# The first unit's softmax by tiles, and a new hand-written order for the opening of an attention and channel-mix kernel

## The chip, the cores and the metric

One core of a Trainium2 chip runs the whole kernel. The metric is the time of one execution in device microseconds, the median of three runs. The profile shows one execution of its own. Engines are named as in the profile: PE (matrix products), DVE (vector), ACT (activations), POOL (GpSimd), SP (the queue that issues the transfers).

## What is computed

Local attention over 4 batches of 768 tokens with 8 heads of 64, then a channel mix on the 512 features of each token:

```
for each chunk of 32 queries:
    k_full = concat(mem_k, k[chunk_start-16 : chunk_end+8])      # v_full the same
    a = softmax(q_chunk @ k_full.T / 8);  out = a @ v_full
x      = out as (batch, 768, 512);  x_prev = x shifted by one token
xk, xr = mu_k*x + (1-mu_k)*x_prev,  mu_r*x + (1-mu_r)*x_prev
k = relu(xk @ w_k);  v = (k*k) @ w_v;  r = sigmoid(xr @ w_r)
return r * v
```

w_k is 512 x 1024, w_v 1024 x 512, w_r 512 x 512; all are given as 64-bit floats.

## The kernel before

The tokens are worked in 12 units of 256, each of two tiles of 128. For a unit `u` the operations carry these names; the tile is `t` = 2u or 2u+1:

- `qk`, `vw`: loads of queries and keys, and of values, of a tile (672 and 512 KB).
- `s`: the scores of both tiles on PE, into one PSUM tile of two banks (line 430). `max`, `sub`, `exp`, `sum`, `norm`: the softmax on all 16 groups of 64 keys at once, each one instruction on 1024 elements per partition (lines 443 to 465; `sum` is a reduction, an addition and a reciprocal). `max` first writes a large negative number over the keys that don't exist at a batch's ends.
- `t`: transposes on PE; `bd.0`, `bd.1`: two copies that spread the transposed weights into a block-diagonal tile; `a`: the product with the values; `x`: the copy into the unit's token matrix `xT`.
- `mix`, `xh`, `xl`: the blend with the shifted tokens, and its split into a high part (fp32r) and a low part. For unit 0 the blend is a product on PE with diagonal matrices (`dg0`, `dg1`, eight ACT instructions each, line 346, from the identity `id` and `mu`). For later units `df` (line 593) takes the difference of a token and its predecessor and `mix` (line 603) does four multiply-adds on DVE for each of the two blends; the second blend is written over `df`.
- `h`, `g`, `v`: the products with w_k, w_r and w_v, each as three products of high and low parts (lines 654, 630). `sig` is the sigmoid of `g`; `relu`, `sq`, `kh`, `kl` the square of the rectified `h` and its split. From unit 3 on (`FAST`) the v product is done in seven parts (line 961) with sums of weights made on DVE.
- `w0` to `w9`: chunks of the weights of 1 MB: 0 and 1 are w_r, 2 to 5 w_k, 6 to 9 w_v. `load`; `mag` (ACT), `low` and `join` (DVE) make 32-bit floats of the 64-bit ones; `hi` and `lo` split them. In unit 0 `h0.n` needs chunk 2+n alone and `g0.n` chunk n alone, so that products start before all weights are there; `v0.n` needs chunk 6+n.

A planner orders everything. Its list `FIRST`, written out by hand, gives the opening operation by operation, each with its engine; each engine and the SP queue do theirs in that order. Behind the list a greedy planner with prices per operation and due times from PE's order goes on. PE's order from unit 1 on is fixed in `te_order`. Buffers are rings with few places: four of `big` (loads of `qk` and weights), six of `x4`, three of `vw`, one score tile `s`, two PSUM banks `tp`, four PSUM banks `m`. Where the planner foresees that PE idles early on, warm-up products on zeros are put in (line 1088).

PE's opening order before is `s0 s1 t0 t1 a0 a1`, `mix0.0 mix0.1 t2 t3 s2 a2 a3`, `h0.0` to `h0.3`, `t4 t5 s3 g0.0 g0.1 a4 a5 g1.0 g1.1`, then `h1` and `v0`.

Of the kernel before, what the change touches and what calls it, by code (L numbers as in the profile page):

```python
# [1139 lines left out]
```

## Time and profile before

| | us |
|---|---|
| runs | 399.12, 399.76, 399.77 (median 399.76) |
| the profiled execution | 398.94 |
| its span, first to last instruction | 397.2 |
| PE busy | 388.1 (98%) |
| DVE busy | 323.2 (81%) |
| ACT busy | 215.2 (54%) |
| POOL busy | 15.9 (4%) |

The span is what the trace covers; 1.74 us of the profiled execution lie around it. The granted clock of TensorE is 1.00 throughout. Busy shares are means over the whole span; the opening, which the change touches, is read from its own stretches.

### The profile page before, as it was taken

What the parts mean: (1) busy time and instruction counts of PE and PEld (TensorE: products, weight loads), DVE (VectorE), ACT (ScalarE), POOL (GpSimd) and SP (SyncE); (2) the same over time, 40 slices, a digit from 0 to 9 for tenths busy, and PEclk for the clock granted to TensorE, in tenths of its full rate; (3) what the DMA queues carried; (4) which work ended last, traced back from release to release, by engine and by line L of the source; (5) the groups of instructions that cost most, each with busy time, mean ns of one, the idle gap of its engine ahead of it and who ended that gap; (6) DMA issues with size and microseconds to landing.
All of it is one profiled execution on the core that took longest, in us unless ns stands there. A gap on an engine that the chain in (4) does not pass through costs nothing.

```text
span 397.2 us, 10852 instructions
## 1 busy us (share of the span) xinstructions
PE 388.1 (98%) x4803; PEld 357.6 (90%) x4803; DVE 323.2 (81%) x561; ACT 215.2 (54%) x340; POOL 15.9 (4%) x14
## 2 busy tenths in 40 slices
PE   7889999999999999999999999999999999999996
PEld 3579889888988989989989989989989999989995
DVE  1888989998789999789879879779779779478446
ACT  1867797714642864457457466357358364344440
POOL 2243020000010000000000000000000000000000
PEclk9999999999999999999999999999999999999999
DMA  8999894011063260142142142142130130100101
GB/s 304 412 352 355 268 362 133 8 69 39 2 229 110 102 246 3 55 151 98 55 138 110 54 174 73 54 148 99 55 109 2 53 108 2 53 2 2 54 0 53
DMA packets 13054, 46.63 MB, mean 117 GB/s; under 512 B 1488, under 2 KB 1872, under 8 KB 12496
## 3 DMA queue, kind: packets, MB, share of 16 engines
q1 hardware_dynamic: 13008, 45.95, 31.9%
q8 instruction: 37, 0.61, 0.6%
q14 instruction: 9, 0.07, 0.1%
HBM read 39.65 MB, written 6.29 MB: 116 GB/s over the span
## 4 chain that ended last, share of the span: by engine, by line
PE 93%; DVE 3%; ACT 2%; DMA 1%; issue 0%; SPq 0%; DVEq 0%
PE ph L654 33%; PE pr L630 17%; PE pv L630 8%; PE pa L961 6%; PE pb L961 6%; PE px L509 6%; PE pc L961 5%; PE s L430 4%; PE pd L961 3%; PE pt L492 3%; PE xf L562 2%; DMA qk<-in_qk_dram 1%; ACT k L346 1%; DVE sm_sb L443 1%; DVE e L447 1%; DVE o L985 0%
## 5 line engine op out<-in xcount | busy, mean ns | idle before, releaser
L654 PE MATMUL ph<-xh,wkh 128*128 128x256 f32 x384 | 106.2, 277 | 0.0
L654 PE MATMUL ph<-xl,wkh 128*128 128x256 f32 x384 | 106.0, 276 | 0.0
L654 PE MATMUL ph<-xh,wkl 128*128 128x256 f32 x384 | 106.0, 276 | 0.0
L654 PEld LDWEIGHTS ph<-xh,wkh 128*128 128x128 f32 x384 | 72.1, 188 | 0.2
L654 PEld LDWEIGHTS ph<-xl,wkh 128*128 128x128 f32 x384 | 72.1, 188 | 0.0
L654 PEld LDWEIGHTS ph<-xh,wkl 128*128 128x128 f32 x384 | 72.1, 188 | 0.0
L742 ACT ACTIVATE k<-ph 128x512 f32<-128x512 f32 x48 | 28.6, 598 | 71.9 <-PE ph L654 71.8
L917 DVE TENSOR_TENSOR khl<-k,khl 128x512 fp32r<-128x512 f32 x63 | 42.2, 687 | 25.4 <-ACT khl L316 24.4
L630 PE MATMUL pr<-wrh,xh 128*128 128x512 f32 x96 | 39.1, 408 | 0.0
L630 PE MATMUL pr<-wrl,xh 128*128 128x512 f32 x96 | 37.6, 392 | 0.0
L630 PE MATMUL pr<-wrh,xl 128*128 128x512 f32 (+1 forms) x108 | 37.6, 366 | 0.0
L316 ACT CAST khl<-k 128x512 fp32r<-128x512 f32 x43 | 26.4, 622 | 7.5 <-PE pb L961 2.5
L630 PE MATMUL pv<-wvh,khl 128*128 128x512 f32 (+1 forms) x97 | 30.3, 389 | 0.0
L749 ACT ACTIVATE k<-k 128x512 f32<-128x512 f32 x47 | 29.5, 632 | 1.3
L509 PEld LDWEIGHTS px<-aTz,vw 128*64 128x64 f32 x768 | 23.4, 138 | 3.4 <-issue 2.4
L509 PE MATMUL px<-aTz,vw 128*64 128x64 f32 x768 | 25.0, 223 | 1.1 <-DVE aTz L318 1.1
L318 DVE CAST khl<-k 128x512 fp32r<-128x512 f32 x32 | 13.1, 423 | 15.6 <-ACT k L749 15.2
L316 ACT COPY aTz<-pt 64x512 f32<-64x512 f32 x34 | 19.1, 580 | 12.0 <-PE pt L492 11.1
L701 ACT ACTIVATE sg<-pr 128x512 f32<-128x512 f32 x24 | 14.3, 599 | 19.4 <-PE pr L630 19.3
L961 PE MATMUL pc<-wtbig,khl 128*128 128x256 f32 x204 | 24.6, 276 | 0.0
L630 PEld LDWEIGHTS pr<-wrh,xl 128*128 128x128 f32 x108 | 20.3, 188 | 4.6
L961 PEld LDWEIGHTS pc<-wtbig,khl 128*128 128x128 f32 x204 | 23.8, 188 | 0.0
(110 smaller groups left out, 757.3 us busy)
## 6 DMA issues: line engine op xcount, KB each, us to landing
qk<-in_qk_dram SPq DMA_DIRECT2D x24, 672.0 KB, 6.1
vw<-in_vw_dram SPq DMA_DIRECT2D x24, 512.0 KB, 4.8
out_dram<-o SPq DMA_DIRECT2D x23, 256.0 KB, 2.1
raw<-in_w_k_dram SPq DMA_DIRECT2D x4, 1024.0 KB, 8.0
raw<-in_w_v_dram SPq DMA_DIRECT2D x4, 1024.0 KB, 6.6
raw<-in_w_r_dram SPq DMA_DIRECT2D x2, 1024.0 KB, 5.9
out_dram<-o SPq DMA_DIRECT2D x2, 128.0 KB, 1.7
id_sb<-in_ident_dram SPq DMA_DIRECT2D x1, 64.0 KB, 6.8
```

What stands on the lines that cost most here:

```text
L316: e.copy(dst, src)
L318: e.tensor_copy(dst, src)
L430: nc.tensor.matmul(s5[CHUNK * j : CHUNK * (j + 1), h, c, r, :], q4[z, r, j, :], k3[z, r, STEP * j : STEP * j + NK], start=True, stop=True,)
L492: nc.tensor.transpose(p[:, n * P : (n + 1) * P], e[:, n // 2, c, n % 2, :], id_sb)
L509: nc.tensor.matmul(p3[64 * h : 64 * h + 64, 2 * g : 2 * g + 2, CHUNK * j : CHUNK * j + CHUNK], v[:, g, h, j, :], a[:, h, g, j, :], start=True,
L630: nc.tensor.matmul(p[:, a : a + step], x, w[:, a : a + step], start=start, stop=stop and a + step == DM)
L654: nc.tensor.matmul(z, w, x[:, k], start=start, stop=stop)
L701: nc.scalar.activation(T["sg", u][:, c * DM : (c + 1) * DM], T["pr", u, c], AF.Sigmoid)
L742: e.activation(r, T["ph", u, f], AF.Relu)
L749: e.activation(q, q, AF.Square)
L917: e.tensor_sub(T["al", u, name], src, T["ah", u, name].bitcast(F32))
L961: nc.tensor.matmul(p, l[:, i], r[i], start=i + k == 0, stop=i == FT // 2 - 1 and k == 2)
```

## The change

Four things change. The softmax of unit 0 is done tile by tile: `s0`, `max0`, `sub0`, `exp0`, `sum0`, `norm0` work on the first tile's eight groups and a second set with the letter b on the other's; the second tile's scores go to the two `tp` banks, in two pieces. Unit 2 (`EACH`) has its exponential in 16 instructions on ACT, one for each group, that take the scaled maximum as bias (`neg2` on DVE makes it) and give the group's sum as well; the subtraction and the reduction are gone. From unit 3 on the blend is made without `df`: four ACT instructions `old` scale the preceding token by 1-mu, for each of the two blends, and four DVE instructions add mu times the token. And `FIRST` is another list: in it the loads of queries and values stand ahead of those of weights, `dg0` and `dg1` stand elsewhere, `norm1` and the low parts of three chunks are on DVE in place of POOL, `x1` is on ACT, and more such. PE's order changes in that `s0b` comes behind `s0`, and `s2` ahead of `t3`. Of the lists the first ten lines are shown.

```diff
+EACH = (2,)
...
 FIRST = """
-qk1@dma qk0@dma s0@pe max0@dve sub0@dve mu@dma w3.load@dma w3.low@dve w3.mag@act w3.join@dve exp0@act sum0@dve id@dma
-norm0@dve dg0@act dg1@act qk2@dma qk3@dma s1@pe t0@pe t1@pe bd0.0@act vw1@dma w3.hi@dve w3.lo@pool bd1.1@act vw0@dma
-bd0.1@dve bd1.0@act w2.load@dma a0@pe a1@pe x0@act max1@dve sub1@dve w2.mag@act x1@dve w2.low@dve w2.join@dve
-mix0.0@pe exp1@act w4.load@dma sum1@dve w4.mag@act xh0.0@act qk4@dma w4.low@dve mix0.1@pe norm1@pool t2@pe xl0.0@dve
-qk5@dma w4.join@dve bd2.1@dve w2.hi@act xh0.1@act vw2@dma bd2.0@act t3@pe bd3.0@act w4.hi@act w2.lo@pool w4.lo@pool
-bd3.1@dve vw3@dma xl0.1@dve w5.load@dma w5.mag@act w0.load@dma s2@pe max2@dve w1.load@dma qk7@dma sub2@dve w5.low@dve
-w5.join@dve w0.low@dve exp2@act sum2@dve vw4@dma a2@pe a3@pe x2@act x3@act w5.hi@act w5.lo@dve h0.0@pe h0.1@pe
-w1.low@dve w0.mag@act h0.2@pe h0.3@pe w1.mag@act qk6@dma w0.join@dve w0.hi@act relu0.0@act norm2@dve t4@pe bd4.0@act
-relu0.1@act sq0.1@act vw5@dma sq0.0@act kh0.0@act t5@pe w0.lo@dve s3@pe g0.0@pe relu0.3@act w1.join@dve w1.hi@dve
-relu0.2@act bd4.1@act bd5.1@act sq0.3@act w7.load@dma w7.mag@act bd5.0@act w1.lo@dve g0.1@pe sq0.2@act a4@pe x4@act
...
+qk0@dma mu@dma id@dma qk1@dma dg0@act s0@pe max0@dve sub0@dve exp0@act s0b@pe max0b@dve sub0b@dve exp0b@act qk3@dma
+qk2@dma vw0@dma vw1@dma w2.load@dma w3.load@dma dg1@act sum0@dve norm0@dve sum0b@dve norm0b@dve s1@pe t0@pe qk5@dma
+qk4@dma vw2@dma bd0.0@act bd0.1@dve t1@pe bd1.0@act bd1.1@dve a0@pe vw3@dma x0@act max1@dve a1@pe x1@act sub1@dve
+mix0.0@pe mix0.1@pe w2.low@dve exp1@act w2.mag@act sum1@dve w3.mag@act w2.join@dve w4.load@dma xh0.0@act norm1@dve
+w2.hi@act w3.low@dve w2.lo@dve w3.join@dve w5.load@dma t2@pe xh0.1@act bd2.1@dve bd2.0@act s2@pe xl0.0@dve t3@pe
+bd3.0@act bd3.1@dve a2@pe w3.hi@act xl0.1@dve x2@act a3@pe w4.mag@act w0.load@dma w1.load@dma w4.low@dve w3.lo@dve
+x3@act w4.join@dve w4.hi@act w5.mag@act max2@dve neg2@dve h0.0@pe w4.lo@dve exp2@act w5.low@dve w5.join@dve qk6@dma
+w5.hi@dve w5.lo@dve h0.1@pe w0.mag@act w0.low@dve h0.2@pe w1.mag@act w1.low@dve sum2@dve vw4@dma norm2@dve w0.join@dve
+h0.3@pe qk7@dma w0.hi@dve t4@pe w0.lo@dve t5@pe w1.join@dve w1.hi@dve relu0.1@act relu0.0@act sq0.0@act vw5@dma
+bd5.1@act bd4.0@act w1.lo@dve df1@dve sq0.1@act s3@pe g0.0@pe g0.1@pe relu0.2@act w7.load@dma mix1.1@dve w6.load@dma
...
+        split = u == 0
+        parts = [[c] for c in range(QPU)] if split else [range(QPU)]
+
+        def groups(cs):
+            n = NG // QPU
+            return slice(n * cs[0], n * (cs[-1] + 1))
+
+        def room(h, c):
+            if split:
+                x = T["s", u, c, h] if c else T["s", u][:, h * 512 : (h + 1) * 512]
+                return x[:, : NPAIR * NK].rearrange("p (r k) -> p r k", k=NK)
+            return T["s", u].rearrange("p (h c r k) -> p h c r k", h=2, c=QPU, r=NPAIR)[:, h, c]
+
+        def pieces(cs):
+            if not split:
+                return [(slice(0, NG), T["s", u].rearrange("p (g k) -> p g k", k=NK))]
+            n, c = NPAIR, cs[0]
+            if c == 0:
+                s = T["s", u].rearrange("p (h x) -> p h x", h=2)[:, :, : n * NK]
+                return [(slice(0, 2 * n), s.rearrange("p h (r k) -> p h r k", k=NK))]
+            return [(slice(n * (2 * c + h), n * (2 * c + h + 1)), room(h, c)) for h in range(2)]
+
+        def f_s(cs):
+            if cs[0] == 0:
+                T["s", u] = ps("s", f"s{u}", QPU)
+            else:
+                for h in range(2):
+                    T["s", u, cs[0], h] = ps("tp", f"s{u}_{h}")
...
+            for c in cs:
+                a = T["qk", ts[c]]
...
+                                room(h, c)[CHUNK * j : CHUNK * (j + 1), r, :], q4[z, r, j, :], k3[z, r, STEP * j : STEP * j + NK],
...
+        def f_max(cs):
+            for c in cs:
+                for h in range(2):
+                    if qts[ts[c]][1] == 0:
+                        nc.vector.memset(room(h, c)[0:CHUNK, :, 0:LEFT], NEG)
+                    if qts[ts[c]][1] == NQT - 1:
+                        nc.vector.memset(room(h, c)[P - CHUNK : P, :, LEFT : LEFT + RIGHT], NEG)
+            T["mx", u], T["sum", u] = sm_sb[:, :NG], sm_sb[:, NG : 2 * NG]
+            for g, s in pieces(cs):
+                mx = T["mx", u][:, g]
+                nc.vector.reduce_max(mx.rearrange("p (h r) -> p h r", h=2) if len(s.shape) == 4 else mx, s, axis=AX.X)
+
+        def f_sub(cs):
+            if cs[0] == 0:
+                T["e", u] = sb("e", [P, NG, NK], f"e{u}")
+            for g, s in pieces(cs):
+                e, mx = T["e", u][:, g], T["mx", u][:, g]
+                if len(s.shape) == 4:
+                    e, mx = e.rearrange("p (h r) k -> p h r k", h=2), mx.rearrange("p (h r) -> p h r", h=2)
+                nc.vector.tensor_sub(e, s, mx.unsqueeze(len(mx.shape)).to_broadcast(list(s.shape)))
+
+        def f_exp(cs):
+            e = T["e", u][:, groups(cs)]
...
+        def f_sum(cs):
+            g = groups(cs)
+            sm = T["sum", u][:, g]
+            nc.vector.reduce_sum(sm, T["e", u][:, g], axis=AX.X)
...
+        def f_neg(cs):
+            mx = T["mx", u][:, groups(cs)]
+            nc.vector.tensor_scalar_mul(mx, mx, -SCALE)
+
+        def f_each(cs):
+            e = T["e", u] = sb("e", [P, NG, NK], f"e{u}")
+            s = T["s", u].rearrange("p (g k) -> p g k", k=NK)
+            for g in range(NG):
+                nc.scalar.activation(
+                    e[:, g], s[:, g], AF.Exp, scale=SCALE, bias=T["mx", u][:, g : g + 1],
+                    accum_out=T["sum", u][:, g : g + 1],
+                )
+
+        def f_rec(cs):
+            sm = T["sum", u][:, groups(cs)]
+            nc.vector.tensor_scalar_add(sm, sm, 1e-9)
+            nc.vector.reciprocal(sm, sm)
+
+        def f_norm(n, cs):
+            e = T["e", u][:, groups(cs)]
+            n.tensor_mul(e, e, T["sum", u][:, groups(cs)].unsqueeze(2).to_broadcast(list(e.shape)))
...
+        norms, z = [], 0.55 if split else 1.0
+        t1 = [Slot("tp") for _ in range(2 * split)]
+        for n, cs in enumerate(parts):
+
+            def on(f, cs=cs):
+                return lambda: f(cs)
+
+            v, first = "b" * n, n == 0
+            o_s = op(f"s{u}{v}", ("pe", 1.4 * z), on(f_s), [l[c] for c in cs] + [prior.get("s")], new=[s1] if first else t1, use=[qs[c] for c in cs], due=ds)
+            o_m = op(f"max{u}{v}", ("dve", 1.17 * z), on(f_max), [o_s], new=[m1] * first, use=[s1, *t1, m1], due=ds + 4)
+            if u in EACH:
+                o_b = op(f"neg{u}", ("dve", 0.2), on(f_neg), [o_m], use=[m1], due=ds + 4.4)
+                o_e = op(f"exp{u}", ("act", 4.3), on(f_each), [o_b], new=[e, m2], use=[s1, m1], table="exp")
+                o_u = op(f"sum{u}", ("dve", 0.45), on(f_rec), [o_e], use=[m2])
+            else:
+                o_b = op(f"sub{u}{v}", ("dve", 1.17 * z), on(f_sub), [o_m], new=[e] * first, use=[s1, *t1, m1, e], due=ds + 5.5)
+                o_e = op(f"exp{u}{v}", ("act", 1.02 * z), on(f_exp), [o_b], use=[e], table="exp")
+                o_u = op(f"sum{u}{v}", ("dve", 1.65 * z, True), on(f_sum), [o_e], new=[m2] * first, use=[e, m2])
+            o_n = op(
+                f"norm{u}{v}", either(dve=(1.14 * z, True), pool=(2.2 * z, True)), lambda g, cs=cs: f_norm(g, cs), [o_u],
+                use=[e, m2],
+            )
+            norms += [o_n] * len(cs)
+            prior.update(s=o_s)
+        return norms, e
...
-            e = T["e", u].rearrange("p (h c g r) k -> p h c g (r k)", h=2, c=QPU, g=2)
+            deal = "(c h g r)" if u == 0 else "(h c g r)"
+            e = T["e", u].rearrange(f"p {deal} k -> p h c g (r k)", h=2, c=QPU, g=2)
...
-        o_t = op(f"t{t}", ("pe", 0.45), f_t, [o_n, o_id, prior.get("t")], new=[s2], use=[e], due=dt)
+        o_t = op(f"t{t}", ("pe", 0.45), f_t, [o_n[c], o_id, prior.get("t")], new=[s2], use=[e], due=dt)
...
+        if u >= FAST:
+            for m in (0, 1):
+                fs = Slot("x4", [0, 1])
+
+                def f_old(m=m, fs=fs):
+                    f = T["xf", u, m] = sb(fs, [P, KT, UTOK], f"xf{u}_{m}")
+                    for k in range(KT):
+                        nc.scalar.activation(
+                            f[:, k], T["xT", u][:, k, :UTOK], AF.Copy, scale=mu_sb[:, m + 2, k : k + 1]
+                        )
+
+                def f_new(m=m):
+                    f = T["xf", u, m]
+                    for k in range(KT):
+                        nc.vector.scalar_tensor_tensor(
+                            f[:, k], T["xT", u][:, k, 1 : 1 + UTOK], mu_sb[:, m, k : k + 1], f[:, k], ALU.mult, ALU.add
+                        )
+
+                o_a = op(f"old{u}.{m}", ("act", 1.5), f_old, deps + [diag[m][0]], new=[fs], use=[xslot[u]])
+                o_d = op(f"mix{u}.{m}", ("dve", 1.9, True), f_new, [o_a], use=[fs, xslot[u]])
+                both(u, m, o_d, fs)
+            return
```

## Rows read from the trace of the kernel before

**Rows 1.** The page, its first part: busy time of each engine, share of the span, instructions.
```profile
PE 388.1 (98%) x4803; PEld 357.6 (90%) x4803; DVE 323.2 (81%) x561; ACT 215.2 (54%) x340; POOL 15.9 (4%) x14
```

**Rows 2.** The span cut into stretches (us from its start). Columns: length, busy time of PE, of its weight loads, of DVE, ACT and POOL with the number of instructions, then the granted TensorE clock, the DMA engines' busy share and GB/s.
```profile
0.00:15.00 15.00, 12.04 (x272) 6.23 (x272) 6.61 (x10) 6.43 (x15) 2.29 (x8) 1.00 0.88 338
15.00:20.00 5.00, 3.87 (x87) 3.05 (x73) 3.85 (x5) 4.24 (x13) 2.36 (x1) 1.00 1.01 420
20.00:25.00 5.00, 3.86 (x28) 3.32 (x24) 4.83 (x8) 3.60 (x4) 0.00 (x0) 1.00 1.01 413
25.00:30.00 5.00, 5.00 (x89) 4.36 (x90) 3.93 (x5) 2.86 (x5) 4.97 (x2) 1.00 0.78 274
30.00:35.00 5.00, 5.00 (x174) 4.84 (x157) 3.80 (x6) 2.96 (x4) 2.86 (x2) 1.00 0.99 389
35.00:40.00 5.00, 5.00 (x47) 5.00 (x46) 4.83 (x8) 4.22 (x7) 0.00 (x0) 1.00 0.90 333
40.00:45.00 5.00, 4.97 (x45) 4.64 (x45) 5.00 (x6) 2.77 (x4) 0.00 (x0) 1.00 0.72 220
45.00:50.00 5.00, 5.00 (x145) 4.29 (x145) 4.93 (x8) 4.89 (x10) 0.00 (x0) 1.00 0.92 320
...
80.00:120.00 40.00, 40.00 (x407) 35.24 (x406) 34.33 (x71) 17.05 (x29) 1.04 (x1) 1.00 0.25 88
120.00:160.00 40.00, 40.00 (x583) 37.33 (x583) 38.74 (x73) 21.77 (x34) 0.00 (x0) 1.00 0.33 111
...
200.00:390.70 190.70, 190.70 (x2249) 181.51 (x2248) 148.61 (x270) 97.72 (x152) 0.00 (x0) 1.00 0.19 67
```

**Rows 3.** The chain of waits that ended last, its first 60 us. Columns: start, length in us, what it was (engine, tile written, line; x is the number of steps).
```profile
1.18 5.48 DMA qk<-in_qk_dram
...
6.70 1.50 PE s L430 x91
...
14.57 2.34 ACT k L346 x8
16.91 0.48 ACT aTz L316
...
17.42 0.69 DVE aTz L318
...
20.70 0.61 DVE xT L318
...
21.44 7.15 PE xf L562 x32
...
32.89 11.08 PE ph L654 x96
...
46.47 5.68 PE pr L630 x25
```

**Rows 4.** Two single issues of the SP queue, the first load of the kernel (issued at 0.75 us) and a load of one weight chunk issued at 28.30 us: KB, and us from issue to landing.
```profile
qk<-in_qk_dram SPq DMA_DIRECT2D x1, 672.0 KB, 4.2
```
```profile
raw<-in_w_r_dram SPq DMA_DIRECT2D x1, 1024.0 KB, 5.0
```

**Rows 5.** DVE's instructions in order of time, from the second unit's maximum to the instruction behind the second weight chunk's low part. Columns: start, length in us, engine, line, operation, tiles, shape; in brackets the idle time before it and what ended it.
```profile
18.14 1.23 DVE L443 TENSOR_REDUCE sm_sb<-s 128x16 f32<-128x1024 f32 x1
...
26.51 1.73 DVE L383 SCALAR_TENSOR_TENSOR mag<-mag,raw 128x1024 uint32<-128x1024 uint32 x1
29.06 0.69 DVE L318 COPY aTz<-pt 64x512 f32<-64x512 f32 x1 [0.82 <-PE pt L492]
30.94 0.69 DVE L318 COPY aTz<-pt 64x512 f32<-64x512 f32 x1 [1.19 <-ACT aTz L316]
...
38.20 1.21 DVE L459 TENSOR_REDUCE sm_sb<-e 128x16 f32<-128x1024 f32 x1
39.44 0.17 DVE L460 TENSOR_SCALAR sm_sb<-sm_sb 128x16 f32<-128x16 f32 x1
...
41.49 1.22 DVE L383 SCALAR_TENSOR_TENSOR mag<-mag,raw 128x1024 uint32<-128x1024 uint32 x1
...
46.97 1.22 DVE L389 TENSOR_TENSOR wrl<-mag,wrh 128x1024 fp32r<-128x1024 f32 x1
48.11 1.22 DVE L593 TENSOR_TENSOR df<-xT 128x1024 f32<-128x1024 f32 x1
```

**Rows 6.** POOL's instructions in order of time, same columns.
```profile
25.02 2.13 POOL L465 TENSOR_TENSOR e<-e,sm_sb 128x1024 f32<-128x1024 f32 x1 [6.11 <-DVE sm_sb L461]
27.12 3.35 POOL L389 TENSOR_TENSOR wkl<-mag,wkh 128x1024 fp32r<-128x1024 f32 x1
```

**Rows 7.** ACT's instructions in order of time: the first set of diagonals, and the small instruction in front of the second.
```profile
12.05 2.43 ACT L346 ACTIVATE k<-id_sb,mu_sb 128x128 f32<-128x128 f32 x8
14.38 0.19 ACT L343 ACTIVATE mu_sb<-mu_sb 128x4 f32<-128x4 f32 x1
```

**Rows 8.** Groups of instructions by line and shape. Columns: count, busy us, mean ns of one, idle time of the engine before them and what ended it. The first three are of the first 120 us, the last of the whole span.
```profile
L759 DVE TENSOR_TENSOR khl<-k,khl 128x512 fp32r<-128x512 f32 x12 | 8.1, 686 | 1.9 <-ACT khl L316 1.9
L346 ACT ACTIVATE k<-id_sb,mu_sb 128x128 f32<-128x128 f32 x16 | 4.9, 387 | 0.0
L593 DVE TENSOR_TENSOR df<-xT 128x1024 f32<-128x1024 f32 x3 | 3.7, 1220 | 0.1
```
```profile
ACT k L742 <- PE ph L654: 71.8, 37, 7.6
```

**Rows 9.** PE's warm-up products (line 1088) in order of time, columns as in rows 5.
```profile
1.06 4.58 PE L1088 MATMUL warm<-zero_sb 128*128 128x512 f32 x6 [1.06 <-DVE zero_sb L305]
...
8.11 4.56 PE L1088 MATMUL warm<-zero_sb 128*128 128x512 f32 x10
```

More of the change, by code (lines that the diff above doesn't have):

```diff
@@ L58 @@
-df1@dve kh0.1@dve mix1.1@dve xh1.1@dve w8.load@dma w8.mag@act xl1.1@dve w6.load@dma a5@pe x5@act w6.mag@act mix1.0@dve
-xh1.0@dve xl1.0@pool sig0.0@act sig0.1@act max3@dve sub3@dve kl0.1@dve w7.low@dve w9.load@dma w9.low@dve w6.low@dve
-w7.join@dve kh0.3@act g1.0@pe g1.1@pe h1.0@pe sig1.0@act sig1.1@act w6.join@dve kl0.0@dve kh0.2@act w9.mag@act
-w9.join@dve w6.hi@act kl0.3@dve exp3@act h1.1@pe w6.lo@dve h1.2@pe relu1.1@act sq1.1@act w7.hi@act w8.low@dve
-w8.join@dve h1.3@pe relu1.0@act kl0.2@dve w9.hi@act relu1.3@act w7.lo@dve sq1.0@act df2@dve w8.hi@act w8.lo@dve
@@ new lines @@
+bd5.1@act bd4.0@act w1.lo@dve df1@dve sq0.1@act s3@pe g0.0@pe g0.1@pe relu0.2@act w7.load@dma mix1.1@dve w6.load@dma
+xh1.1@dve xl1.1@dve mix1.0@dve bd4.1@act relu0.3@act bd5.0@act sq0.2@act kh0.1@act kh0.2@act w8.load@dma kh0.0@act
+a4@pe sig0.0@act sig0.1@act kl0.1@dve kl0.0@dve w7.low@dve xh1.0@act xl1.0@dve w8.low@dve w7.mag@act w6.mag@act
+w9.load@dma w6.low@dve w7.join@dve w6.join@dve a5@pe g1.0@pe g1.1@pe h1.0@pe sq0.3@act kh0.3@act h1.1@pe kl0.3@pool
+x4@dve w7.hi@act x5@dve max3@dve sub3@dve sig1.0@act w7.lo@pool kl0.2@dve relu1.0@act sig1.1@act w6.hi@act df2@dve
@@ L64 @@
+w8.mag@act sq1.0@act w9.low@dve w6.lo@dve h1.2@pe h1.3@pe relu1.2@act relu1.1@act w9.mag@act relu1.3@act sq1.2@act
+v0.0@pe w8.join@dve w9.join@dve sq1.3@act w8.hi@act mix2.1@dve v0.1@pe exp3@act w9.hi@act w8.lo@dve v0.2@pe kh1.0@dve
+kl1.0@dve sq1.1@act w9.lo@dve kh1.1@act kl1.1@dve xh2.1@act xl2.1@dve mix2.0@dve kh1.2@act kl1.2@pool v0.3@pe
 """
@@ L582, in mixed, with both, f_hi, f_lo @@
             mix[0, m] = (o_h, o_l, hs, ls)
+    def both(u, m, o_d, fs):
+        def f_hi(e):
+            h = T["xh", u, m] = split_x(f"xh{m}", f"xh{u}_{m}", m)
+            copy(e, h, T["xf", u, m])
+        def f_lo(e):
+            l = T["xl", u, m] = split_x(f"xl{m}", f"xl{u}_{m}", m)
+            e.tensor_sub(l, T["xf", u, m], T["xh", u, m].bitcast(F32))
+        hs, ls = Slot(f"xh{m}"), Slot(f"xl{m}")
+        o_h = op(f"xh{u}.{m}", either(act=(1.0,), dve=(0.61, True)), f_hi, [o_d], new=[hs], use=[fs])
+        o_l = op(f"xl{u}.{m}", either(dve=(1.14, True), pool=(2.4, True)), f_lo, [o_h], new=[ls], use=[fs, hs])
+        mix[u, m] = (o_h, o_l, hs, ls)
     def prep(u):
@@ L605, in f_mix @@
                     )
[L607 to L615 removed]
             o_d = op(f"mix{u}.{m}", ("dve", 1.6, True), f_mix, [o_d, o_mu], new=[fs] if n == 0 else [], use=[ds, xslot[u]])
[L617 to L619 removed]
+            both(u, m, o_d, fs)
     def channel_mix(u):
```

49 lines of the change are left out of this document (removed).

## Prediction

> **What bounds the kernel now.** The page's busy row comes first: PE is busy for 388.1 of 397.2 us [rows 1], so only PE's time can move the end. The stretches tell where PE isn't full: before 25 us it is idle by some 5 us and otherwise fed with warm-up products; from 25 us to 390.7 us it has 5.00 of 5.00, 40.00 of 40.00, 190.70 of 190.70 (one stretch reads 4.97) [rows 2]. The clock column is 1.00 throughout. So the time is: the start of the first `mix0` product on PE, plus PE's list from there, plus a tail on DVE and the last store. The chain of waits says what sets that start: the second of two query loads lands at 6.66 us, then scores, maximum, subtraction, exponential, both sets of diagonals on ACT, a copy, the second unit's maximum and subtraction on DVE in front of the last copy `x1`, and `mix0` at 21.44 us. After it there is nothing but PE [rows 3]. The reader is to see a second thing in the stretches: DVE has 4.83, 3.93, 3.80, 4.83, 5.00 and 4.93 of 5.00 us between 20 and 50 us, while ACT has 2.8 to 4.9 [rows 2]. DVE is close behind PE as the second bound, and an earlier PE runs into it.
>
> The sum is made against the profiled execution (398.94 us, 1.74 around its span); the median of the three runs is 0.82 us above it, and I carry differences over to the median. From no change a difference of about 0.2%, 0.8 us, can be told.
>
> **The front, step by step.** The first load lands 4.2 us after its issue at 0.75 [rows 3, 4], so 5.0. `s0` is now half the products (1.50 / 2): 5.8. `max0` is two small memsets and 512 elements; 512 elements take 0.69 [rows 8], together about 1.0: 6.9. `sub0` 0.69: 7.6. `dg0` (2.43 [rows 7]) runs on ACT meanwhile, from 5.2, as ident and mu now stand behind one load. `exp0` about 0.6: 8.3. The second load (0.69 MB at the 0.40 MB/us of a full queue [rows 2]) lands at 6.9, `s0b` ends at 7.7, `max0b` and `sub0b` are two pieces of 256 each: 9.3. Then `sum0` 1.15, `norm0` 0.69, `sum0b`, `norm0b`: 12.9. `s1` needs 2.8 MB, there at 10 to 11, and ends at 12.0 to 12.5, so `t0` starts there and `t1` at 13.0. The two halves of a diagonal copy follow one another: in before the DVE half of a copy waited 1.19 us for ACT's [rows 5]. So `bd0.0`, `bd0.1`, `bd1.0`, `bd1.1` end at 15.0, `a1` at 16.1, `x1` (now on ACT) at 16.8, and `mix0` starts at 17.0: 4.4 us sooner than 21.44.
>
> PE's list behind it is the same work in almost the same order (`s2` and `t3` change places, nothing is added). In before `g0.1`, the second half of the first gate, starts 27.87 us after `mix0` (46.47 + 2.84 = 49.31 [rows 3]). Alone PE would reach it at 44.9.
>
> **What DVE gives back.** `g0.1` needs `w1.lo`, the last piece of the second weight chunk, and DVE works off its list in order. In before DVE goes from `max1` (18.14) to the end of `w1.lo`'s step (48.11) in 29.97 us [rows 5]; `w1.lo` is there 1.1 us before PE wants it. The same stretch of the new list:
> - added: `norm1` (1.14 a step; on POOL before), `w2.lo`, `w3.lo`, `w4.lo` (3 x 1.14; on POOL before), `w3.low` and `w3.join` (0.61 + 1.14; before they stood ahead of `max1`), `w5.hi` and `w0.hi` (2 x 0.61; on ACT before), `neg2` 0.17. Together 7.70.
> - gone: `x1` 0.61, `sub2` 1.14, the reduction of `sum2` 1.24. Together 2.99.
> - waits of before that have no reason now: 0.82 and 1.19 in front of the copies of `t2` and `t3`, and 0.50 by which one join was stretched (1.73 against 1.23) while POOL worked [rows 5, 6]. Together 2.51.
> - new waits: `sum1` behind `exp1` about 0.55, and four more pairs in which an instruction needs the one just ahead of it (0.13 each, the overlap of 0.09 and 0.04): 1.05.
>
> So 29.97 + 7.70 - 2.99 - 2.51 + 1.05 = 33.2 us. `max1` starts at 15.0, when `bd1.1` is done, so `w1.lo` ends at 48.2: the same time as before, though PE is ready 3.3 us earlier. PE spends that in small waits: for the copies of `t2` and `t3` 0.6, for `w5.lo` about 1, for `w0.lo` about 0.8, the rest before `g0.1`. `g0.1` starts at 48.2 instead of 49.31: **1.1 us**. Behind it PE's list is unchanged, `xh1.1` waits for `g0.1` as before, and with the same steps `w6.lo` to `w9.lo` come about 0.9 us ahead of `v0.0` to `v0.3`: in that part of the list DVE gives `w7.lo` and `kl0.3` to POOL (1.75) and takes `x4`, `x5` and `xl1.0` (2.36). So 399.76 - 1.1 = 398.6.
>
> Bounds: the 33 instructions alone, without any wait, are 16 x 1.14, 11 x 0.61, two of 1.2, 1.3, 1.6, 0.4 and 0.17, 30.8 us: `w1.lo` at 45.8, a gain of 3.4 us. With waits as long as before's 2.5 kept and a front 0.5 us later it ends at 50.6: a loss of 1.3 us. I stand near the middle, as only the waits I can name are counted.
>
> **The loads.** w3 goes from fourth place in SP's queue to tenth, behind four loads of queries, two of values and w2. The bytes ahead of w2, w3 and w4's ends are 4.9, 6.0 and 9.4 MB; 5.07 had come by 15 us, 7.17 by 20, 9.24 by 25 [rows 2], and up to 2 us more in a full queue: 17, 19 and 27.6, each ahead of its `mag`. w5 is issued when `w3.join` is done (25.4) and takes 5.0 alone [rows 4]: 30.4, before DVE asks at 34. w0, w1 and qk6 wait behind it on SP. qk7 waits for `w5.join` (36.8) and lands at 41.8, 0.5 us before `s3`; without that cover each us costs one only beyond the wait for `w0.lo`. Cost: nothing.
>
> **Unit 2's exponential by slices.** Sixteen ACT instructions of 64 elements with a pointer bias and an accumulated sum replace one of 1.06. No row shows the accumulated form. From below: eight of 128 elements with a pointer scale take 2.43, a step of 0.29 [rows 7], so at most 0.29 and 4.7 us without the accumulator. From above: the whole 0.387 [rows 8] plus a whole small instruction of 0.19, unpipelined: 0.58 and 9.2 us. The room is from `neg2` (33.7) to `sum2`'s place on DVE (40.0), 6.3 us, 0.39 a slice. The nearest row is the 0.29, so I take no cost. If it is longer, `sum2` holds DVE, and behind it `norm2`, `w0.join`, `w0.lo`, `w1.join`, `w1.lo` and with them PE.
>
> On this the Trainium skill has a rule that speaks against the change (Perfetto Trace Analysis, Optimizing Scalar/DVE Operations): each Scalar or DVE instruction pays a fixed data access of its own, about 93 ns for Scalar on SBUF, so fewer and larger operations are better on a full engine. By it the fifteen extra instructions would cost an estimated 1.4 us of ACT time, which no run here shows yet and which would still fit.
>
> **Units 3 to 11.** Each loses `df` (1.22 on DVE [rows 8]) and gets eight ACT instructions of 256 elements with a pointer scale, about 0.4 each: 3.2 us of ACT. PE never waits in these stretches [rows 2], so the DVE time saved is worth nothing, and ACT, which waited 71.8 us for PE in front of the first activations alone [rows 8], covers its 3.2 of 30 us. Were that cover gone, a late activation would hold a PSUM bank by up to 1.5 us a unit.
>
> **The rivals.**
> - DVE doesn't hold PE: its waits vanish and `w1.lo` comes near the bare sum, 45.8. Gain 2.2 to 3.4, 396.4 to 397.6. For it: ten of its 33 steps depend only on loads long landed. Against it: weights are joined on DVE from ACT's pieces, and DVE had waits in every stretch so far.
> - It changes nothing: a front 0.5 us later (`qk2` at 11.2, and `s0` at the pace of PE's first products: six warm-up products took 4.58 us at the start and ten took 4.56 later, with a granted clock of 1.00 in both [rows 2, 9]) and 0.5 us more waits on DVE. `w1.lo` at 49.2, time 399.0 to 400.5.
> - Slower: a slice of unit 2's exponential takes more than 0.39 us. Then each 0.1 us holds DVE by 1.6. From 0.46 the gain is gone, from 0.51 the kernel is over 0.2% slower; at 0.58 it ends near 401.7. For it: the accumulator's write has no row. Against it: the step of the pointer form is 0.29.
> - Slower, later: ACT's extra 3.2 us a unit makes PE wait in units 3 to 11. At 0.3 us each it is 2.7 us, 401.3. Against it: ACT is at about half.
>
> **How the numbers follow.** The forecast (gain 0 to 2.2 us, most likely 1.1) has 0.5, DVE out of the way 0.15, no change 0.17, the long slices 0.12, the later waits 0.06. Faster by over 0.2%: two thirds of the forecast and all of the first rival, 0.5. Within 0.2%: the rest of the forecast and the no-change case, 0.31. Slower: 0.19. The likeliest case's own range is 397.6 to 399.8. For 8 in 10, half of the first rival and half of the slower ones stay out: 396.7 to 400.8.
>
> **What would show it.** Right: `mix0` near 17.0, `w1.lo` on DVE ending near 48.2, `g0.1` directly behind it, PE idle for some 3 us in all between 24 and 48, full from then on. Wrong: `mix0` after 18; `sum2` waiting for ACT at 40 us; PE idle behind 55 us; a slice step above 0.39.

## The result, and the profile after

The changed kernel takes 402.07 us (median of five executions, 401.58 to 403.73) against 399.2 before (median of five, run beside it): a ratio of 1.008, interval 1.0065 to 1.0096. It is slower by some 3 us; the forecast was 398.6, a gain of 1.1. The profiled execution is one of 403.73 us. The five executions lie at two levels: three between 401.6 and 402.1 with a mean granted clock of 0.996 to 1.00, two near 403.6 with 0.990. The second level is part of the finding, below.

The busy row and the stretches of the kernel after, columns as in [rows 1, 2]:

```profile
PE 390.3 (97%) x4797; PEld 359.0 (89%) x4797; DVE 316.6 (79%) x570; ACT 247.1 (61%) x442; POOL 13.0 (3%) x13
```
```profile
4.00:5.00 1.00, 0.95 (x21) 0.16 (x28) 0.00 (x0) 0.02 (x1) 0.00 (x0) 1.00 1.07 186
5.00:6.00 1.00, 1.00 (x65) 0.83 (x54) 0.15 (x2) 1.00 (x4) 0.00 (x0) 1.00 0.87 204
6.00:7.00 1.00, 0.75 (x2) 0.00 (x0) 0.93 (x3) 1.00 (x5) 0.00 (x0) 1.00 0.89 360
...
10.00:15.00 5.00, 2.91 (x89) 1.47 (x89) 4.69 (x12) 3.06 (x10) 0.00 (x0) 0.98 1.02 419
15.00:20.00 5.00, 4.22 (x77) 3.68 (x79) 2.02 (x3) 1.26 (x3) 0.00 (x0) 0.50 1.00 377
20.00:25.00 5.00, 5.00 (x55) 4.21 (x53) 3.74 (x5) 3.50 (x5) 0.00 (x0) 0.83 0.91 349
...
80.00:120.00 40.00, 40.00 (x388) 35.12 (x389) 34.75 (x69) 21.08 (x34) 2.87 (x2) 1.00 0.16 59
120.00:160.00 40.00, 40.00 (x588) 36.61 (x584) 36.10 (x69) 28.68 (x53) 2.40 (x1) 1.00 0.43 140
...
200.00:395.00 195.00, 195.00 (x2281) 185.53 (x2281) 145.66 (x272) 117.24 (x203) 0.00 (x0) 1.00 0.19 66
```

From 55 us to the end PE is as full as in [rows 2], with 31.9 us more ACT work and 6.6 less on DVE over the span. Everything was lost ahead of that. Two things stand out: between 4 and 6 us the transfers moved 186 and 204 GB/s, half of what a full queue moves, and from 15 to 20 us TensorE's granted clock was 0.50, its 1.2 GHz level.

The chain of waits of the kernel after, its first 24 us (columns as in [rows 3]), and the issue of the second query load (as in [rows 4]):

```profile
2.11 6.93 DMA qk<-in_qk_dram
9.04 0.04 issue
9.08 0.90 PE s L457 x53
...
12.43 1.06 PE s L457 x62
13.49 1.69 issue
15.18 0.92 PE s L457 x40
16.10 1.90 PE pt L559 x8
18.00 0.59 issue
18.59 3.46 PE px L576 x64
22.05 1.05 PE warm L1180 x2
23.11 6.91 PE xf L629 x32
```
```profile
qk<-in_qk_dram SPq DMA_DIRECT2D x1, 672.0 KB, 6.9
```

The second query load lands at 9.04, not 6.9; `s1` is broken off for 1.69 us in which PE waits for nothing that the profile shows; the transposes take 1.90 us and the value products 3.46, against 1.04 and 2.08 us for the same counts in the trace of before, because the clock is at its lower level; `mix0` starts near 23 instead of 17.0 (before: 21.44 [rows 3]).

DVE from the second unit's maximum to the last piece of the second weight chunk (columns as in [rows 5]):

```profile
19.37 1.23 DVE L472 TENSOR_REDUCE sm_sb<-s 128x16 f32<-128x1024 f32 x1
...
23.67 1.22 DVE L490 TENSOR_REDUCE sm_sb<-e 128x16 f32<-128x1024 f32 x1 [1.19 <-ACT e L485]
...
33.16 0.69 DVE L320 COPY aTz<-pt 64x512 f32<-64x512 f32 x1 [0.59 <-ACT aTz L318]
...
46.02 0.17 DVE L509 TENSOR_SCALAR sm_sb<-sm_sb 128x16 f32<-128x16 f32 x1
...
52.76 1.23 DVE L391 TENSOR_TENSOR wrl<-mag,wrh 128x1024 fp32r<-128x1024 f32 x1
```

`max1` starts at 19.37 and `w1.lo` ends at 53.99; the first product that reads it starts at 54.04.

Unit 2's slices on ACT, first and last pair, and the group of the blend's new ACT instructions over the whole span (as in [rows 8]):

```profile
40.06 0.31 ACT L502 ACTIVATE e<-s,sm_sb 128x64 f32<-128x64 f32 x1
40.26 0.20 ACT L502 ACTIVATION_READ_ACCUMULATOR e<-s,sm_sb 128x1 f32 x1
...
44.41 0.40 ACT L502 ACTIVATE e<-s,sm_sb 128x64 f32<-128x64 f32 x1
44.61 0.30 ACT L502 ACTIVATION_READ_ACCUMULATOR e<-s,sm_sb 128x1 f32 x1
44.70 2.32 ACT L378 ACTIVATE mag<-raw 128x1024 f32<-128x1024 f32 x2
```
```profile
L676 ACT ACTIVATE xf<-xT,mu_sb 128x256 f32<-128x256 f32 x72 | 30.0, 497 | 1.9 <-DVE xT L320 1.7
```

Sixteen slices from 40.06 to 44.70 are 0.29 us each, although each is two instructions; DVE came to `sum2` at 46.02 without waiting for them.

### The profile page after: what moved, and what is told of

The parts are those of the page before. It is cut to its first block, busy times and chain, and to the rows that moved or that the text cites. A ratio compares the mean times of both kernels' runs of the same rounds, so it can differ in the third digit from the quotient of the medians.

```text
span 401.9 us, 10947 instructions
## 1 busy us (share of the span) xinstructions
PE 390.3 (97%) x4797; PEld 359.0 (89%) x4797; DVE 316.6 (79%) x570; ACT 247.1 (61%) x442; POOL 13.0 (3%) x13
## 4 chain that ended last, share of the span: by engine, by line
PE 90%; DVE 5%; DMA 3%; issue 1%; SPq 0%; ACT 0%; ACTq 0%
PE ph L746 30%; PE pr L722 16%; PE pv L722 8%; PE pa L1053 6%; PE px L576 6%; PE pb L1053 6%; PE pc L1053 5%; PE s L457 4%; PE pt L559 3%; PE pd L1053 3%; DMA qk<-in_qk_dram 2%; PE xf L629 2%; DMA vw<-in_vw_dram 2%; DVE mag L385 1%; DVE wrl L391 1%
## 5 line engine op out<-in xcount | busy, mean ns | idle before, releaser
L318 ACT CAST khl<-k 128x512 fp32r<-128x512 f32 x45 | 27.6, 620 | 7.6 <-PE pb L1053 2.7
L676 ACT ACTIVATE xf<-xT,mu_sb 128x256 f32<-128x256 f32 x72 | 30.0, 497 | 1.9 <-DVE xT L320 1.7
L683 DVE SCALAR_TENSOR_TENSOR xf<-xT,mu_sb,xf 128x256 f32<-128x256 f32 x72 | 29.9, 476 | 0.0
L576 PEld LDWEIGHTS px<-aTz,vw 128*64 128x64 f32 x768 | 24.9, 144 | 3.6 <-issue 2.2
L576 PE MATMUL px<-aTz,vw 128*64 128x64 f32 x768 | 26.6, 230 | 1.0 <-issue 0.6
L318 ACT CAST xh<-xf 128x1024 fp32r<-128x1024 f32 (+1 forms) x22 | 21.2, 963 | 6.9 <-DVE xf L683 5.1
L457 PEld LDWEIGHTS s<-qk 64*32 64x32 f32 x1536 | 16.2, 106 | 10.2 <-issue 5.0
```

The lines of the kernel that those rows point to most:

```text
L318: e.copy(dst, src)
L457: nc.tensor.matmul(room(h, c)[CHUNK * j : CHUNK * (j + 1), r, :], q4[z, r, j, :], k3[z, r, STEP * j : STEP * j + NK], start=True, stop=True,)
L576: nc.tensor.matmul(p3[64 * h : 64 * h + 64, 2 * g : 2 * g + 2, CHUNK * j : CHUNK * j + CHUNK], v[:, g, h, j, :], a[:, h, g, j, :], start=True,
L676: nc.scalar.activation(f[:, k], T["xT", u][:, k, :UTOK], AF.Copy, scale=mu_sb[:, m + 2, k : k + 1])
L683: nc.vector.scalar_tensor_tensor(f[:, k], T["xT", u][:, k, 1 : 1 + UTOK], mu_sb[:, m, k : k + 1], f[:, k], ALU.mult, ALU.add)
```

## The experiments

Four theories come first: F, the front failed (second query load late, lower clock); D, DVE's longer list alone sets the time and the front is worth nothing; S, the slices hold DVE; L, the later units' extra ACT work costs. Later ones are named in the texts written before each run. All runs below were timed against the kernel before, which took 398.98 to 399.23 beside them. Of the lists' long lines only the part that matters is shown, with dots where it is cut; an operation that moves is gone from its old place.

**The second query load ahead of the small ones.**

```diff
-qk0@dma mu@dma id@dma qk1@dma dg0@act s0@pe ...
+qk0@dma qk1@dma mu@dma id@dma dg0@act s0@pe ...
```

> The changed kernel, but the second load of queries stands ahead of mu and ident in the SP queue (qk0, qk1, mu, id). Theory F (the front): what the change lost is its front. The second load landed at 9.04 us, not at 6.9, and everything up to mix0 is late by it. Then here qk1 lands near 6.7, mix0 on PE starts about 2 us sooner than the changed kernel's 23.1, and the time falls by 1.5 to 2.5 us, to about 399.5 to 400.5. Theory D (DVE's longer list): the front is worth nothing, since w1.lo on DVE sets the gate product; time unchanged within 0.5 us of the changed kernel's. The diagonals dg0 start later here (mu and ident behind 0.7 MB more), which by F costs at most the 0.7 us by which exp0 then waits.

Measured: 399.78 us, ratio 1.002 (1.0011 to 1.0030). Transfers between 4 and 6 us, and DVE at both ends of its stretch:

```profile
4.00:5.00 1.00, 0.92 (x29) 0.22 (x33) 0.00 (x0) 0.00 (x0) 0.00 (x0) 1.00 1.04 430
5.00:6.00 1.00, 0.64 (x64) 0.48 (x44) 0.21 (x2) 0.00 (x0) 0.00 (x0) 1.00 1.00 372
```
```profile
10.08 0.69 DVE L490 TENSOR_REDUCE sm_sb<-e 128x8 f32<-128x512 f32 x1 [1.29 <-ACT e L485]
...
16.39 1.23 DVE L472 TENSOR_REDUCE sm_sb<-s 128x16 f32<-128x1024 f32 x1
...
48.48 1.23 DVE L391 TENSOR_TENSOR wrl<-mag,wrh 128x1024 fp32r<-128x1024 f32 x1
```

The load lands at 6.40, the clock stays at 1.00, `max1` starts 2.98 us sooner, and 2.3 us of the median come back. F holds for that much, and D falls. `id` now lands at 7.06, so `exp0` waits behind `dg0`: the 1.29 us.

**More warm-up products**, so that PE idles less before `t0`.

```diff
+                n += {"s0b": 2, "s1": 1, "a0": 1}.get(o.name, 0)
```

> The changed kernel with four more warm-up products on PE: two ahead of s0b, one ahead of s1, one ahead of a0 (each 0.86 us at full clock). Theory F: part of the front's loss is that PE idled 2.3, 0.6 and 1.9 us before 15.2 us and the granted clock then was 0.50 from about 15 to 22 us. Then the clock reads 1.00 in all executions here, transposes and value products take 0.9 and 2.0 us and not 1.9 and 3.5, and the time is that of the changed kernel's executions with a clock of 1.00 (401.6) in every run, not 403.6. Theory D: the clock is without effect, as DVE holds the gate product anyway; the same two times as before, 401.6 to 403.7.

Measured: 401.96 us (401.88 to 402.14), ratio 1.0071 (1.0056 to 1.0086). The stretch in which the clock had been 0.50:

```profile
15.00:20.00 5.00, 4.62 (x123) 3.67 (x123) 2.87 (x5) 1.75 (x4) 0.00 (x0) 1.00 0.98 384
```

With the second load still late (9.26), `max1` starts at 18.53 and `w1.lo` ends at 52.29: the lower clock is 1.7 us of the profiled execution of after. None of the four executions is at the 403.6 level; four are too few to show that the warm-ups did it, as two of after's five fell.

**Unit 2's softmax as before.**

```diff
-EACH = (2,)
+EACH = ()
...
-x3@act w4.join@dve w4.hi@act w5.mag@act max2@dve neg2@dve h0.0@pe ...
+x3@act w4.join@dve w4.hi@act w5.mag@act max2@dve sub2@dve h0.0@pe ...
```

> The changed kernel with unit 2's softmax as before (one subtraction, one exponential, one reduction in place of 16 slices). Theory F: DVE gets 2.3 us back on a list that sets the start of g0.1, so w1.lo ends about 2 us later and the time is 1.5 to 2.5 us longer, near 404. Theory S (the slices hold DVE at sum2): the time falls by 1 us or more, to 400.5 or less.

Measured: 404.62 us, ratio 1.014 (1.0123 to 1.0157). That is 2.5 us above after. In the profiled execution DVE's stretch from `max1` to the end of `w1.lo` is 35.8 us, where it is 33.5 to 33.8 in the versions with the slices and a clock that stayed up: 2.0 to 2.3 more, for a subtraction and a reduction that came back and a `neg2` that went (1.14 + 1.24 - 0.17 = 2.2 in the prediction's terms). S falls: the slices are worth their whole DVE time. What DVE does ahead of `w1.lo` counts one for one. Another 0.5 us lies behind `w1.lo` (table below) and has no cause here.

**The blend of units 3 to 11 as before**: the branch for `u >= FAST` in the blend is taken out.

> The changed kernel with the blend of units 3 to 11 as before (difference and multiply-adds on DVE, no scaling on ACT). Theory F: PE is full from 55 us on in both, so the time is the changed kernel's within 0.5 us. Theory L (the later units): ACT's 3.2 us a unit cost PE waits, so the time falls by 1 us or more.

Measured: 402.87 us (401.87 to 404.16), ratio 1.0095 (1.0068 to 1.0121), with executions at the same two levels as after: 401.87 and 402.11 at a clock of 1.00 (after: 401.58 and 401.64), 403.63 and 404.16 at 0.99 (after: 403.57 and 403.73). Neither level is shorter with the old blend, so L falls.

**The same gap in the kernel before.** There the small loads are moved between the two query loads.

```diff
-qk1@dma qk0@dma s0@pe max0@dve sub0@dve mu@dma w3.load@dma w3.low@dve w3.mag@act w3.join@dve exp0@act sum0@dve id@dma
+qk1@dma mu@dma id@dma qk0@dma s0@pe max0@dve sub0@dve w3.load@dma w3.low@dve w3.mag@act w3.join@dve exp0@act sum0@dve
```

> The kernel before with one thing changed: the two small loads, mu and id, are issued between the first and the second qk tile, as the kernel after has them (before: mu behind both, id behind w3). Theory H (small transfers between two large ones on one queue leave a hole behind them, wherever they stand): the second qk tile lands at about 9.0 instead of 6.65, s0, which wants both, begins at 9.1 instead of 6.70, all up to mix0 follows by 2.3 to 2.4 us (mix0 at 23.7), and the time rises to 401 to 401.5. Rival N (the late landing belongs to something else that the kernel after does): the second tile lands by 7.0 and the time stays at 399 to 399.3.

Measured: 400.88 us, ratio 1.0045 (1.0029 to 1.0062). The window of the transfers, the issue of the second query load, then a later stretch:

```profile
4.00:5.00 1.00, 1.00 (x2) 0.46 (x2) 0.00 (x0) 0.00 (x0) 0.00 (x0) 1.00 1.23 214
5.00:6.00 1.00, 1.00 (x2) 0.00 (x0) 0.00 (x0) 0.00 (x0) 0.00 (x0) 1.00 0.68 258
```
```profile
qk<-in_qk_dram SPq DMA_DIRECT2D x1, 672.0 KB, 6.0
```
```profile
10.00:15.00 5.00, 5.00 (x9) 2.21 (x10) 4.75 (x6) 3.34 (x7) 0.00 (x0) 0.76 0.92 334
```

The gap is there (before: 414 and 396 in the same two microseconds), and the second query tile lands at 8.13 instead of 6.65; theory H had 9.0, so its kind is right and its size too large. `mix0` starts at 24.09, 2.65 us later, of which the lower clock from about 9 to 12.4 us is a part. The median rises by 1.65 us.

**The small loads on ACT's queue.**

```diff
-    o_id = op("id", ("dma", 0.2), lambda: nc.sync.dma_start(id_sb, ident))
-    o_mu = op("mu", ("dma", 0.1), lambda: nc.sync.dma_start(mu_sb[:, 0:2], mu))
+    o_id = op("id", ("dma", 0.2), lambda: nc.scalar.dma_start(id_sb, ident))
+    o_mu = op("mu", ("dma", 0.1), lambda: nc.scalar.dma_start(mu_sb[:, 0:2], mu))
```

> The kernel after with mu and id issued from ACT's queue instead of SP's, nothing else changed, so that qk0 and qk1 stand back to back on SP's queue. Theory H (the late landing of qk1 comes from its place behind the small transfers on its own queue): qk1 lands at about 6.5 instead of 9.04 and the time falls by the 2.3 us that a_loads gained, to 399.5 to 400. Rival M (it is the size of the small packets, whatever queue they are on): qk1 lands after 8 and the time stays at 401 to 402.

Measured: the second query load lands at 6.68, as theory H has it; M falls. Five executions with a clock of 0.999 to 1.00 took 399.17 to 399.84, five with 0.989 to 0.992 took 402.0 to 403.5, so the median is 400.93 (ratio 1.0039, 1.0008 to 1.0071): late loads aren't needed for the clock to fall. What made it fall in half of these executions stays open; the trace is of one in which it did not, and a version below whose loads land as early kept 0.998 to 1.00 in all ten. In the profiled one (399.17, clock 1.00) `max1` starts at 15.94.

**The small loads first, both diagonal steps first on ACT.**

```diff
-qk0@dma mu@dma id@dma qk1@dma dg0@act s0@pe ...
+mu@dma id@dma qk0@dma qk1@dma dg0@act dg1@act s0@pe ...
```

> The kernel after with the two small loads ahead of both qk tiles (mu, id, qk0, qk1) and both diagonal steps, dg0 and dg1, first on ACT's list, where ACT otherwise idles. Theory G (only the front failed; from max1 on the forecast's sums hold): the diagonals end before exp0, qk0 and qk1 land by 5.2 and 6.9, max1 starts near 15.0, mix0 near 17.5, w1.lo ends 33.3 later, at 48.3, and the time is 398.4 to 398.6, just below before. Rival J (the gap behind small transfers only moves: qk0 now follows them and starts late): qk0 lands after 6.5 and qk1 after 8, max1 near 16.5 or later, the time 400 or more.

Measured: 400.35 us, ratio 1.0027 (1.0004 to 1.0050). The query loads land at 5.79 and 7.51, between the two expectations, `max1` starts at 16.89 and `w1.lo` ends at 50.37: rival J's outcome. The front of the forecast isn't reached this way either.

**The diagonal steps later on ACT.** In the first of two kernels `dg0` goes behind `exp0b`, in the second `dg1` too, behind `bd1.0`; both have `qk1` ahead of the small loads.

```diff
-... dg0@act s0@pe max0@dve sub0@dve exp0@act s0b@pe max0b@dve sub0b@dve exp0b@act qk3@dma
+... s0@pe max0@dve sub0@dve exp0@act s0b@pe max0b@dve sub0b@dve exp0b@act dg0@act qk3@dma
...
-... bd1.0@act bd1.1@dve ...
+... bd1.0@act dg1@act bd1.1@dve ...
```

> The kernel of a_loads (qk1 ahead of mu and id) with dg0 moved on ACT's list from ahead of exp0 to behind exp0b. In a_loads DVE idled 1.29 us before the first sum, for exp0 behind dg0, and 0.66 and 0.60 at the two copies behind ACT's. Theory C (in the first 55 us the time is the start of max1 on DVE plus a stretch of 33.3 us to the end of w1.lo): sum0 begins near 8.8, max1 near 15.1, w1.lo ends near 48.4 and the time falls 1.3 us, to 398.5. Rival A (ACT only moves the wait: bd0.0 and bd1.0 now stand behind dg0 and dg1): max1 stays at 16.2 to 16.4, the time at 399.7.

> As a_dg (qk1 ahead of mu and id, dg0 behind exp0b) with dg1 moved behind bd1.0, so that ACT's two copies no longer wait for both diagonal steps; in a_dg DVE idled 2.51 us for them. Theory C (time = start of max1 + 33.3 us): bd0.0 at 13.7, max1 near 15.4, w1.lo ends near 48.7, the time is 398.9. Rival X (dg1 then holds x0 and x1, and mix0 and exp1 with them): mix0 at 19 or later, DVE waits at sum1 for exp1, and the time stays at 399.5 to 399.9.

Measured: the first 399.84 us, ratio 1.0019 (1.0005 to 1.0032); DVE's 1.29 us of waiting shrinks to nothing and 2.51 us appear further on, in front of the copies behind ACT's, so `max1` starts at 16.62: rival A. The second 399.25 us, ratio 1.000 (0.998 to 1.0021):

```profile
14.29 1.30 DVE L320 COPY aTz<-pt 64x512 f32<-64x512 f32 x2 [1.64 <-ACT aTz L318]
15.62 1.23 DVE L472 TENSOR_REDUCE sm_sb<-s 128x16 f32<-128x1024 f32 x1
...
48.14 1.22 DVE L391 TENSOR_TENSOR wrl<-mag,wrh 128x1024 fp32r<-128x1024 f32 x1
```

`max1` starts at 15.62 and `w1.lo` ends at 49.36. Theory C is right within 0.4 us in the time and 0.7 in the end of `w1.lo`, and this is the best version found. It doesn't beat the kernel before.

**Work from DVE to POOL.** On top of the first of these, `norm1@pool` for `norm1@dve`, then also `w3.lo@pool` for `w3.lo@dve`.

> As a_dg, with norm1 on POOL instead of DVE. Theory C: DVE's stretch is shorter by norm1's 1.2 us, w1.lo ends near 47.2 and the time is 397.3. Rival T (norm1 on POOL takes over 2 us and t2, bd2 and xl0 wait for it, so DVE idles for what it saves): the same as a_dg within 0.3 us.

> As a_dg_p1, with w3.lo on POOL too. Theory C: another 1.2 us off DVE's stretch, w1.lo ends near 46 and the time is 396.1; by then PE's own work (27.9 us from mix0 to g0.1 in the kernel before) is nearly the bound, with mix0 near 17.2 to 18.5 it allows g0.1 at 45.1 to 46.4. Rival W (the hidden products wait for the slower POOL): PE waits for w3's lower half in h0, g0.1 comes later by that wait, 397.3 or more.

Measured: 400.42 us, ratio 1.0031 (1.0018 to 1.0044), and 400.90 us, ratio 1.0038 (1.0024 to 1.0053). Neither gains: DVE's stretch is 33.9 and 34.1 us, against 33.5. Both expectations of theory C fail, and the waits that the rivals name aren't there either. DVE and POOL of the kernel with `norm1` on POOL, and the same DVE instruction with `norm1` on DVE:

```profile
22.69 2.39 DVE L381 TENSOR_SCALAR raw<-raw 128x1024 uint32<-128x1024 uint32 x1
```
```profile
21.86 2.66 POOL L514 TENSOR_TENSOR e<-e,sm_sb 128x1024 f32<-128x1024 f32 x1 [18.92 <-DVE sm_sb L492]
```
```profile
24.07 0.70 DVE L381 TENSOR_SCALAR raw<-raw 128x1024 uint32<-128x1024 uint32 x1
```

While POOL worked from 21.86 to 24.52, DVE's instruction issued at 22.69 ended only at 25.08: 2.39 us instead of 0.70. DVE got rid of 1.13 us and was stretched by 1.7. In the other kernel `w3.lo` on POOL stretched another instruction of the same line to 1.85. In the kernel before the same thing showed as a join of 1.73 us [rows 5, 6]. The Trainium skill (SBUF — State Buffer, SBUF: two separate sides) states a rule for this: GpSimd's instructions and some of DVE's (those in a mode that takes two ports, or with two inputs in SBUF) share one pair of ports as an exclusive lock, held for a whole instruction, and the other engine blocks. The trace agrees, with 2.39 against 0.70.

**A product moved into PE's wait.** On top of the version with both diagonal steps later, `a4` goes between `g0.0` and `g0.1`.

```diff
-... bd4.0@act w1.lo@dve df1@dve sq0.1@act s3@pe g0.0@pe g0.1@pe ...
+... bd4.0@act bd4.1@act w1.lo@dve df1@dve sq0.1@act s3@pe g0.0@pe a4@pe g0.1@pe ...
```

> As a_dg1, with a4 moved on PE's list from behind g0.1 to between g0.0 and g0.1, and bd4.1 on ACT's list ahead for it. In a_dg1 PE finishes g0.0 about 0.8 us before w1.lo ends (49.36) and idles at g0.1; a4 is 1.9 us of products. Theory C (PE's wait for w1.lo is what still costs): the wait is filled, g0.1 ends at the same place but a4 lies behind PE already, and the time falls by 0.7 to 0.9 us, to 398.4. Rival B (bd4.1, and the first unit's gate values, come later for it and the sigmoid and the next products follow): no gain, 399.2 or more.

Measured: 400.04 us, ratio 1.0034 (1.0016 to 1.0052). Rival B's outcome, at another place than it named: behind the moved product DVE waits for the gate's end, and PE then for DVE (0.3 us).

```profile
53.30 0.70 DVE L320 CAST xh<-xf 128x1024 fp32r<-128x1024 f32 x1 [0.72 <-PE pr L722]
```

There was also less to fill than the 0.8 us of the expectation. In the version without the move PE's last product ahead of `w1.lo` starts at 48.92 and the first that reads it at 49.41; the products around them follow one another every 0.23, so PE waits 0.26. Of the 0.8 us between the two medians the profiled executions show 0.37 in a later `max1` and 0.3 behind `w1.lo`; three of the twelve executions were at a clock of 0.990 or 0.991 and took 402.1 to 402.5.

**All of them side by side.** From the profiled executions: start of `max1`, end of `w1.lo`, the time of that execution, and what lies between the last two.

| kernel | max1 | to w1.lo's end | w1.lo ends | time | rest |
|---|---|---|---|---|---|
| after | 19.37 | 34.6 | 53.99 | 403.73 | 349.7 |
| more warm-ups | 18.53 | 33.8 | 52.29 | 401.99 | 349.7 |
| unit 2 as before | 18.52 | 35.8 | 54.31 | 404.53 | 350.2 |
| blend as before | 18.71 | 33.5 | 52.18 | 401.87 | 349.7 |
| qk1 ahead | 16.39 | 33.3 | 49.71 | 399.43 | 349.7 |
| small loads first | 16.89 | 33.5 | 50.37 | 400.05 | 349.7 |
| small loads on ACT's queue | 15.94 | 33.5 | 49.42 | 399.17 | 349.7 |
| dg0 later | 16.62 | 33.5 | 50.09 | 399.97 | 349.9 |
| dg0, dg1 later | 15.62 | 33.7 | 49.36 | 399.07 | 349.7 |
| norm1 on POOL | 16.36 | 33.9 | 50.24 | 400.01 | 349.8 |
| norm1, w3.lo on POOL | 16.47 | 34.1 | 50.59 | 400.32 | 349.7 |
| dg0, dg1 later, a4 moved | 15.99 | 33.8 | 49.74 | 399.77 | 350.0 |

In every kernel with the new list the time is the end of `w1.lo` plus 349.7 to 350.2 us. In the kernel before it isn't: there `w1.lo` ends at 48.19 and PE comes to `g0.1` at 49.31, 349.6 us ahead of the end. The bound passed from PE to DVE; that part of the forecast holds in every row.

## Why the prediction was wrong, point by point

- **The second query load** is the step that failed first. The prediction took 0.69 MB at the rate of a full queue and 6.9 us. It landed at 9.04, as two small transfers stood ahead of it in the queue. Taking them away gave 6.40 and 6.68, putting them there in the kernel before gave 8.13. The row to be wary of was the rate itself: it was read from stretches of 5 us in which large transfers follow one another [rows 2].
- **`s1`, the transposes and the value products.** The clock was read as 1.00 throughout [rows 2] and kept. In the new front PE idled 2.33 us for the second load and 1.69 us inside `s1`, and the granted clock was at 0.50 from about 15 to 22 us: 1.7 us, in two of the five executions of after. That `s1` ends at 12.0 to 12.5, as soon as its loads allow, is a second step that failed, and it failed in every version: PE breaks off inside `s1` for 0.15 to 1.69 us, and goes on 5.9 to 6.4 us after the start of `s0b`. Where neither ACT nor the clock comes in between (seven of the twelve traces with the new list), `max1` starts 3.2 to 3.3 us after that. In the best version the break is 0.90 us and `s1` ends at 13.05; without it, an estimate from these two numbers, it would end at 12.15, as forecast. So the late load counts through `s1` too, and a lower clock ahead of the break costs little: with unit 2 as before it was 0.50 from about 9 to 12.6 us, `s1` began later, the break was 0.82, and `max1` at 18.52 is as early as with more warm-ups.
- **The diagonal steps.** That ACT would do `dg0` under the wait for scores holds in after, where `id` lands at 5.12. With the loads mended ACT is in the way in two places: `exp0` behind `dg0` (1.29 us in front of DVE's first sum, with `qk1` ahead) and the copies behind both steps (2.51, with `dg0` later). With both steps later, or both first, it isn't: there DVE waits 1.64 and 2.18 us at the copies, but ACT itself waits 1.46 and 4.43 for PE's transposes, which come behind `s1`. The prediction's `max1` at 15.0 was never reached; 15.62 was the best.
- **What DVE gives back**, 33.2 us from `max1` to `w1.lo`: right. It measured 33.3 to 33.8 wherever the clock stayed up and the list was the new one; 34.6 in the profiled execution of after, where `sum1` waited 1.19 instead of 0.55.
- **PE's part.** `g0.1` directly behind `w1.lo` at 54.04: right in kind. From `mix0` to there PE took some 31 us instead of 27.87. Its idle time between 24 and 55 us is 1.6, not some 3; its weight loads wait 2.7 us for DVE's pieces, part of that while products still run.
- **The loads of weights**: none was waited for. **The slices**: 0.29, as taken from the pointer form, and no hold on DVE; the bound of 0.58 was far off. ACT's time for this exponential rose from 1.06 to 4.64 us, 3.6 more and not the 1.4 of the estimate, and fitted still. **Units 3 to 11**: 497 ns an instruction instead of 0.4, 3.3 us of ACT a unit, and no wait of PE behind 55 us.
- **The sum.** `w1.lo` at 53.99 instead of 48.2 is 5.8 us: 4.4 in the start of `max1`, of which 2.1 is the late load, about 0.8 the clock and most of the rest the break in `s1`, and 1.4 in the stretch, of which 0.8 is the clock. That is nearly the whole difference between 403.7 and the 397.8 (398.94 - 1.1) that the forecast meant for a profiled execution. The forecast's gain was 1.1 us with a front 4.4 us sooner; each microsecond of that front counted in full, so its first 1.1 us of error took the whole gain. The prediction's case of no change had only 0.5 us of it. One of its bounds doesn't come out as written: a `max1` at 15.5, 33.2 us and 2.5 us of waits make 51.2, not 50.6; the measured 53.99 lies beyond both.

That the late load, the list on DVE and the lower clock are the causes of the loss is shown by the runs. Why the clock fell in some executions and not in others, and why `s1` is broken off, is open; the last section has what the traces tell of both.

## What to carry to other kernels

When a step is moved to the head of a queue, price the transfers behind it from the landing of that very one, not from the mean rate: a small transfer between two large ones can cost more than its bytes. Find the one pair, "last piece ready" and "first product that wants it", from which the rest of the time is constant, and check in each version which of the two comes later; here 349.7 to 350.2 us behind it told every outcome. And before work goes to an idle engine, see in the trace what that engine's instructions did to the lengths of the other's.
